# An attention-and-two-MoE kernel on one core: one subtraction put ahead of a weight decode, and three operand splits per token pair put earlier

## The chip, the cores and the metric

The kernel runs on 1 core of one Trainium2 chip. The metric is the device time of one execution in microseconds (us). The engines are called by the names of the profile: PE (TensorE, matmuls), PEld (its weight loads), DVE (VectorE), ACT (ScalarE), POOL (GpSimd) and SP (SyncE, which issues most transfers). Each engine works through its own queue in the order in which the program issues instructions.

## The reference

```python
def _attn_ref(q, k, v, alpha):            # 4 x 8 heads, 768 steps, 48 wide
    for t in range(S):
        state = alpha[:, :, t, :, None] * state + np.einsum('bhd,bhe->bhde', k[:, :, t], v[:, :, t])
        y[:, :, t] = np.einsum('bhd,bhde->bhe', q[:, :, t], state)

def _moe_ref(x, w_in, w_out):             # 3072 x 384, 384 x 2048, 2048 x 384
    h = x @ w_in
    return (h * sigmoid(h)) @ w_out

def _moe2_ref(x, w_gate, w_val, w_out):   # 384 x 1536 twice, 1536 x 384
    g = x @ w_gate
    return (g * sigmoid(g) * (x @ w_val)) @ w_out
```

The output of the attention is the x of the first layer, whose result is the x of the second.

## The kernel before, in words

**Precision.** Matmuls run on fp32r operands. To keep fp32 accuracy an operand is split in a high part (an ACT copy that rounds to fp32r) and a low part (a subtraction source minus high, `sub`, line 321). A product of two split operands is three matmuls: high by high, low by high, high by low.

**First phase (to about 537 us).** Chunks of 128 tokens go through the attention; seven blocks of 3 or 4 chunks go through the first layer in steps (j, f) of block j and 128 hidden columns f. Each step has `g1` (line 721 to 724: h = x times w_in), `act1` (line 733: ACT computes silu twice, line 738 into the high part gh and line 739 in place into the PSUM bank h; the low part gl = h - gh is a DVE subtraction, issued by the `rest` that act1 returns) and `g2` (lines 770, 771 with gh, then 773 with gl). The weights arrive as 64-bit numbers and are decoded on DVE in three instructions (lines 93, 98, 103), rounded on ACT (line 702), and their low part is subtracted on POOL for the first six units and on DVE from then on (`low_unit`). One call of `units1` (line 1298) pushes one unit through one stage each of this chain. Steps are software-pipelined: g1 of step s + 1 is issued ahead of g2 of step s.

**Second phase.** The second layer works on three pairs of 512-token blocks (p = 0, 1, 2). Its gate and value products use a bilinear scheme with 15 products instead of 18 for a 3 by 2 tile of blocks, in eight groups a pair (even groups gate, odd groups value). A group's products p0 to p14 are three matmuls each (line 1095) into accumulators A to K, one PSUM bank each; DVE merges (line 1106) add banks and saved copies in between. For example `"h": ("H", "D", ALU.add, 1)` is H = D + temps 1, and products p10 and p13 both add to D, one before and one after that merge; `"k2"` is K = temps 3 - E, and product p11 then adds to K. In a gate group the operations u0 to u5 are a silu on ACT (line 1122), in a value group the product of the value with that silu on DVE (line 1127), which leaves a tile a per hidden block f and token block b.

**Output.** For each of the 24 (f, b) of a pair, `osplit` (line 1137) makes the high part of a on ACT (line 1147) and the low part on DVE (line 322, by `sub`), and `og` (line 1149) issues nine matmuls (line 1158) with weights from a ring. Operands 0, 1, 3, 4, ... take tiles of the tags gh and gl, two buffers each, which the silus of the second phase also use; every third operand (2, 5, ...) takes the one tile of tag y3. `output` (line 1164) copies finished sums into a tile of tag big2 and writes them out.

**Order of the second phase.** Nothing is reordered by a scheduler: the constants GATE, VALUE, OUTPUT, SPLIT and MOVING give each operation a due time in a scale of 192 per pair and 15 per group, all events are sorted by it (line 1202), and `run` issues them in this order to every engine's queue. The due times are not microseconds. In pair 0 the events around the change are, in order: u2 of group 6 (92.56, ACT), s12 (93.39, ACT), h7 (94.81, an ACT copy for the next pair), C4 of group 6 (95.36, DVE), u4 of group 6 (95.47, ACT, reads what C4 wrote), u5 of group 6 (96.75, ACT), then of group 7 h (97.25, DVE), p13 (98.12), p4 (98.42), u0 (98.46, DVE), g (99.15, DVE), k (100.76, DVE), u3 (101.26, DVE), p3 (101.30), k2 (101.33, DVE), p6, p8, t (102.01, DVE), h9 (102.05, ACT, next pair), u1 (102.14, DVE), p11 (102.34), u2 (102.54, DVE), the high and low part of operand 0 (102.55), p1 (103.21), those of operand 1 (103.89), og 0 (105.43), s11, C4, u4, C5, u5 (108.30 to 110.59), the high and low part of operand 2 (111.12), of operand 3 (112.71), og 1 and og 2 (112.82, 112.83). Pairs 1 and 2 have the same order, 192 and 384 later; pair 2 has no copies for a next pair.

Of the kernel before, what the change touches and what calls it, by code (L numbers as in the profile page):

```python
# [11 lines left out]
F32R = mybir.dt.float32r  # L12
# [49 lines left out]
SPLIT = (  # L62
    102.55, 103.89, 111.12, 112.71, 118.27, 118.43, 119.02, 126.43, 129.94, 131.62, 132.60, 135.86, 138.65,
    143.41, 148.72, 149.46, 154.12, 157.35, 162.20, 163.22, 165.39, 165.58, 174.69, 175.51,
)
MOVING = (
# [202 lines left out]
def fast(ctx, tc, pk, w1, w2, out, bad_i):  # L269
# [5 lines left out]
    blocks1, n = [], 0  # L275
# [20 lines left out]
    mp = ctx.enter_context(tc.tile_pool(name="mp", bufs=2))  # L296
# [24 lines left out]
    def sub(eng, lo, src, hi):  # L321
        eng.tensor_tensor(out=lo, in0=src, in1=hi.bitcast(F32), op=ALU.subtract)  # L322
# [403 lines left out]
    def g1(s):  # L726
        j, f = steps[s]
        w = len(blocks1[j]) * C
        h_t[j, f] = bank(s % 2, f"h{j}_{f}")[:, :w]
        xk = [(x_t[j][:, 0, k, :w], x_t[j][:, 1, k, :w]) for k in range(KT)]  # L730
        product(h_t[j, f], unit_t["1", 2 * f], xk)

    def act1(j, f):
        w = len(blocks1[j]) * C
        hb = h_t.pop((j, f))
        gh = mp.tile([128, 512], F32R, tag="gh", name=f"gh{j}_{f}")[:, :w]
        gl = mp.tile([128, 512], F32R, tag="gl", name=f"gl{j}_{f}")[:, :w]
        ACT.activation(out=gh, in_=hb, func=AF.Silu)  # L738
        ACT.activation(out=hb, in_=hb, func=AF.Silu)  # L739
        act_t[j, f] = (gh, gl)  # L740

        def rest():
            sub(DVE, gl, hb, gh)

        return rest
# [57 lines left out]
    def load_x1(p):  # L803
        r = x1r_t[p] = big(0, f"x1r{p}").rearrange("p (b k t) -> p b k t", b=2, k=KT)
        for b in range(2):
            t = 1024 * p + 512 * b
            SP.dma_start(out=r[:, b], in_=x1_d[:, :, t:t + 512])

    def moving(p, op, eng=None):

        x = x1r_t[p].rearrange("p b k t -> p (b k) t")
        if op[0] == "a":
            out, a, alu, b = SUMS[op]
            (eng or DVE).tensor_tensor(out=x[:, out], in0=x[:, a], in1=x[:, b], op=alu)
            return
        i = int(op[1:])
        if op[0] == "h":
            t = mov[i] = pools2["s"].tile([128, 2, 512], F32R, tag=f"mov{i}", name=f"mov{p}_{i}", bufs=1)
            ACT.activation(out=t[:, 0], in_=x[:, SOURCE[i]], func=AF.Copy)
        else:  # L820
            sub(eng or DVE, mov[i][:, 1], x[:, SOURCE[i]], mov[i][:, 0])
# [313 lines left out]
    o_t, ahl, ob_t, result = {}, {}, {}, {}  # L1135

    def osplit(p, n, low):
        f, b = order[n]
        if low:
            ah, al = ahl[f, b]  # L1140
            return sub(DVE, al, a_t.pop((f, b)), ah)
        if n % 3 == 2:
            y = mp.tile([128, 2, 512], F32R, tag="y3", name=f"ahl{p}_{n}", bufs=1)
            ahl[f, b] = y[:, 0], y[:, 1]
        else:
            ahl[f, b] = [mp.tile([128, 512], F32R, tag=t, name=f"{t}{p}_{n}") for t in ("gh", "gl")]
        ACT.activation(out=ahl[f, b][0], in_=a_t[f, b], func=AF.Copy)  # L1147

    def og(p, n):
        f, b = order[n]  # L1150
        if f == 0:
            for m in range(KT):
                hold((p, b, m), f"o{p}_{b}_{m}", 1)
            o_t[b] = [held[p, b, m][1] for m in range(KT)]
        ah, al = ahl.pop((f, b))
        for m in range(KT):
            for i, (l, x) in enumerate(((0, ah), (1, ah), (0, al))):
                PE.matmul(  # L1158
                    o_t[b][m], part(ring_t[p, f], m, l), x, start=(f == 0 and i == 0),
                    stop=(f == NF2 - 1 and i == 2),  # L1160
                )
        used(p, NG2 + f // 5)

    def output(p, b, m):
        t = 1024 * p + 512 * b
        if b == 0 and m == 0:
            ob_t[p] = mp.tile([128, 2, KT, 512], F32, tag="big2", name=f"ob{p}", bufs=1)
        ob, src = ob_t[p][:, b], o_t[b][m]
        rows = slice(m * 128, (m + 1) * 128)
        end = p == NPAIR - 1 and b  # L1170
        if end and m == 0:
            result["bad"] = nc.values_load(bad_i[0:1, 0:1], min_val=0, max_val=128)
        if end and m == KT - 1:
            ACT.activation(out=ob[:, m, :256], in_=src[:, :256], func=AF.Copy)
            DVE.tensor_copy(ob[:, m, 256:], src[:, 256:])
            for i, eng in enumerate((ACT, SP)):
                cs = slice(256 * i, 256 * i + 256)
                eng.dma_start(out=out[rows, t + cs.start:t + cs.stop], in_=ob[:, m, cs])
        else:
            if m % 2:  # L1180
                DVE.tensor_copy(ob[:, m], src)
            else:
                ACT.activation(out=ob[:, m], in_=src, func=AF.Copy)
            SP.dma_start(out=out[rows, t:t + 512], in_=ob[:, m])
        release((p, b, m))

    events = []
    for p in range(NPAIR):
        t0 = PAIR * p
        for n in range(NG2):  # L1190
            events += [(t0 + GROUP * n + t, lambda a=(p, n, op): group_op(*a)) for op, t in (GATE, VALUE)[n % 2]]
        for n, (f, b) in enumerate(order):
            events.append((t0 + OUTPUT[n], lambda a=(p, n): og(*a)))
            events.append((t0 + SPLIT[n], lambda a=(p, n, 0): osplit(*a)))
            events.append((t0 + SPLIT[n] + 0.004, lambda a=(p, n, 1): osplit(*a)))
            if f == NF2 - 1:
                for m in range(KT):
                    events.append((t0 + OUTPUT[n] + 0.002 + 0.001 * m, lambda a=(p, b, m): output(*a)))
        if p + 1 < NPAIR:
            events.append((t0 + 3 * GROUP, lambda a=p + 1: load_x1(a)))  # L1200
            events += [(t0 + t, lambda a=(p + 1, op): moving(*a)) for op, t in MOVING]
    events.sort(key=lambda e: e[0])
# [95 lines left out]
    def units1(ahead=4, top=NU1):  # L1298


        up_to("s1", st["h1"] - 1, lambda u: low_unit(("1", u), DVE if u >= 6 else POOL), NU1)
        up_to("h1", st["f1"] - 1, lambda u: high_unit(("1", u), wp, "w"), NU1)
        up_to("e1", st["d1"] - 1, lambda u: decode_unit(("1", u), 1), NU1)
        up_to("d1", st["d1"], lambda u: decode_unit(("1", u), 0), min(top, st["l1"]))
        up_to("f1", st["e1"] - 1, lambda u: decode_unit(("1", u), 2), NU1)
        up_to("l1", st["d1"] + ahead - 1, load1, NU1)
# [61 lines left out]
    steps = turns + [(0, f) for f in range(FB, NF1)]  # L1368
    steps += [(j, f) for j in range(2, NB1) for f in range(NF1)]

    due, n = [first] * (2 * len(turns)), first
# [93 lines left out]
    units1()  # L1465
    attn(1, False)
    g1(0)
    rest = act1(*steps[0])
    units1()
    rest()  # L1470
    for s, (j, f) in enumerate(steps):
        need1(2 * f + 1)
        if s == 0:
# [1 line left out]
        n = 19 + 2 * (s + 3 - len(steps))  # L1475
# [25 lines left out]
@with_exitstack  # L1501
def tile_kernel(ctx, tc, pk, w1, w2, out):
    nc = tc.nc
    fp = ctx.enter_context(tc.tile_pool(name="fp", bufs=1))
    bad128 = fp.tile([128, 1], I32, name="bad128")
    with ExitStack() as inner:
        inner.enter_context(tc.manual_schedule())
        rv = fast(inner, tc, pk, w1, w2, out, bad128)
    with tc.If(rv > 0):
        general(tc, pk, w1, w2, out)  # L1510
# [70 lines left out]
```

## Time and profile before

| | |
|---|---|
| median of 3 runs | 937.41 us (936.27 to 938.69) |
| time of the profiled execution | 938.12 us |
| its span, first to last instruction | 936.3 us |
| mean granted TensorE clock | 0.992 |
| PE / PEld busy | 98% / 83% |
| DVE / ACT / POOL busy | 66% / 48% / 31% |
| chain that ended last | PE 89%, DVE 5%, issue 2% |

Times in a timeline row are the start and the duration in us; "xN" is the number of instructions merged into the row, and the brackets at its end give the idle time of the engine ahead of it and what ended it. Instructions of one engine are pipelined, so the next one may start before the last has ended. Ends of matmuls are modelled, starts are recorded.

### The profile page before, as it was taken

The page shows a single profiled execution, that of the slowest core. Times are in us where ns is not written, and L with a number is a line of the kernel's source. Part 1 is how long each engine was busy: PE and PEld are TensorE (multiplying, and loading weights), DVE is VectorE, ACT ScalarE, POOL GpSimd, SP SyncE. Part 2 cuts the span into 40 slices and gives each one's busy share as a digit, 9 for nine tenths or more (in the row PEclk, how much of TensorE's full clock was granted, in tenths as well). Part 3 has the DMA queues.
Part 4 walks back from the last instruction along what each step waited for, and adds up shares of the span by engine and source line. Part 5 has one row for each costly group of instructions (what it writes and reads, how often), then busy time and mean ns, then how long its engine had stood idle before and what let it go on. Part 6 is the DMA issues. An engine that isn't in the chain of part 4 may idle for free.

```text
span 936.3 us, 14380 instructions
## 1 busy us (share of the span) xinstructions
PE 915.2 (98%) x5210; PEld 779.6 (83%) x5210; DVE 618.1 (66%) x1107; ACT 453.0 (48%) x1019; POOL 287.9 (31%) x401
## 2 busy tenths in 40 slices
PE   9989999999999999999999999999999999999996
PEld 5669998889999998988888888878888888888785
DVE  8889936656577668465268366786477875577732
ACT  3545435646465565555346344543544454444432
POOL 5430006528779789686228000000000000000000
PEclk9899999999999999999999999999999999999998
DMA  7854203243645554532375486532757503755302
GB/s 235 300 187 153 85 1 105 80 142 119 194 160 194 167 175 161 181 108 101 118 264 208 157 299 224 185 114 85 244 213 267 194 10 135 269 205 214 121 0 71
DMA packets 43007, 150.89 MB, mean 161 GB/s; under 512 B 4400, under 2 KB 9008, under 8 KB 40240
## 3 DMA queue, kind: packets, MB, share of 16 engines
q1 hardware_dynamic: 42304, 149.30, 46.3%
q8 instruction: 43, 0.70, 0.3%
q10 hardware_dynamic: 624, 0.59, 0.2%
q14 instruction: 36, 0.29, 0.1%
HBM read 118.03 MB, written 29.88 MB: 158 GB/s over the span
## 4 chain that ended last, share of the span: by engine, by line
PE 89%; DVE 5%; issue 2%; DMA 1%; POOL 1%; ACT 1%; SPq 0%; ACTq 0%; POOLq 0%; DVEq 0%
PE o L1158 15%; PE h L721 7%; PE x L773 7%; PE x L770 7%; PE x L771 7%; PE h L722 7%; PE h L724 7%; PE A L1095 5%; PE D L1095 5%; PE E L1095 5%; PE yd L562 2%; PE K L1095 2%; PE F L1095 2%; PE C L1095 2%; PE B L1095 2%; PE G L1095 2%
## 5 line engine op out<-in xcount | busy, mean ns | idle before, releaser
L322 DVE TENSOR_TENSOR gl<-h,gh 128x384 fp32r<-128x384 f32 (+1 forms) x112 | 68.5, 612 | 89.8 <-ACT h L739 84.4
L721 PE MATMUL h<-x,w 128*128 128x384 f32 (+1 forms) x336 | 122.7, 365 | 1.8 <-DMA x<-y 1.8
L770 PE MATMUL x<-gh,w 128*128 128x384 f32 (+1 forms) x336 | 121.5, 362 | 0.4 <-ACT gh L738 0.4
L771 PE MATMUL x<-gh,w 128*128 128x384 f32 (+1 forms) x336 | 121.2, 361 | 0.0
L722 PE MATMUL h<-x,w 128*128 128x384 f32 (+1 forms) x336 | 120.9, 360 | 0.0
L738 ACT ACTIVATE gh<-h 128x384 fp32r<-128x384 f32 (+1 forms) x112 | 59.9, 534 | 105.3 <-PE h L724 103.4
L1158 PE MATMUL o<-gh,ring 128*128 128x512 f32 x288 | 88.8, 389 | 0.0
L773 PE MATMUL x<-gl,w 128*128 128x384 f32 (+1 forms) x336 | 84.5, 359 | 1.6 <-DVE gl L322 1.6
L724 PE MATMUL h<-x,w 128*128 128x384 f32 (+1 forms) x336 | 84.3, 358 | 0.0
L420 POOL TENSOR_TENSOR kq<-in,r 128x256 f32<-128x256 f32 x47 | 43.0, 915 | 130.1 <-DVE rc L419 76.3
L721 PEld LDWEIGHTS h<-x,w 128*128 128x128 f32 x336 | 63.1, 188 | 10.6 <-issue 5.4
L770 PEld LDWEIGHTS x<-gh,w 128*128 128x128 f32 x336 | 63.1, 188 | 6.7 <-ACT gh L738 1.1
L773 PEld LDWEIGHTS x<-gl,w 128*128 128x128 f32 x336 | 61.3, 188 | 8.1 <-DVE gl L322 2.3
L771 PEld LDWEIGHTS x<-gh,w 128*128 128x128 f32 x336 | 63.1, 188 | 5.2
L722 PEld LDWEIGHTS h<-x,w 128*128 128x128 f32 x336 | 63.1, 188 | 5.1
L724 PEld LDWEIGHTS h<-x,w 128*128 128x128 f32 x336 | 61.3, 188 | 5.9
L1158 PEld LDWEIGHTS o<-gh,ring 128*128 128x128 f32 x288 | 54.1, 188 | 11.2
L739 ACT ACTIVATE h<-h 128x384 f32<-128x384 f32 (+1 forms) x112 | 59.5, 532 | 0.0
L322 DVE TENSOR_TENSOR gl<-a,gh 128x512 fp32r<-128x512 f32 x48 | 32.9, 692 | 37.3 <-ACT gh L1147 36.2
L1158 PE MATMUL o<-gl,ring 128*128 128x512 f32 x144 | 56.4, 392 | 0.8 <-DVE gl L322 0.8
L1095 PE MATMUL A<-mov,ring 128*128 128x512 f32 x198 | 55.7, 389 | 0.0
L1095 PE MATMUL D<-mov,ring 128*128 128x512 f32 x198 | 55.6, 389 | 0.0
(211 smaller groups left out, 1983.3 us busy)
## 6 DMA issues: line engine op xcount, KB each, us to landing
ring<-comb_d SPq DMA_DIRECT2D x21, 1920.0 KB, 7.7
raw<-in_w_dram SPq DMA_DIRECT2D x58, 384.0 KB, 4.4
in<-in_pk_dram SPq DMA_DIRECT2D x22, 770.5 KB, 4.4
ring<-wo_d SPq DMA_DIRECT2D x6, 1920.0 KB, 7.3
comb_d<-area SPq DMA_DIRECT2D x8, 896.0 KB, 5.4
in_v<-in_pk_dram SPq DMA_DIRECT2D x24, 256.0 KB, 3.7
comb_d<-area SPq DMA_DIRECT2D x8, 640.0 KB, 4.9
x1r<-x_d SPq DMA_DIRECT2D x6, 768.0 KB, 8.9
```

Of the source, the lines that this page charges most:

```text
L322: eng.tensor_tensor(out=lo, in0=src, in1=hi.bitcast(F32), op=ALU.subtract)
L420: KF(d).tensor_tensor(out=kq_t[d][:, 0], in0=in_t[n][1][:, 0, ps_], in1=r_t[d][:, :, 1:], op=ALU.mult)
L721: PE.matmul(acc, part(u, k), xh, start=(k == 0), stop=False)
L722: PE.matmul(acc, part(u, k, 1), xh, start=False, stop=False)
L724: PE.matmul(acc, part(u, k), xl, start=False, stop=(k == len(xk) - 1))
L738: ACT.activation(out=gh, in_=hb, func=AF.Silu)
L739: ACT.activation(out=hb, in_=hb, func=AF.Silu)
L770: PE.matmul(x1_t[j][m], part(u, m), gh, start=(f == 0), stop=False)
L771: PE.matmul(x1_t[j][m], part(u, m, 1), gh, start=False, stop=False)
L773: PE.matmul(x1_t[j][m], part(u, m), gl, start=False, stop=(f == NF1 - 1))
L1095: PE.matmul(acc, s(hs, r), x[:, hx], start=op in new and i == 0, stop=i == 2, skip_group_check=True,)
L1158: PE.matmul(o_t[b][m], part(ring_t[p, f], m, l), x, start=(f == 0 and i == 0), stop=(f == NF2 - 1 and i == 2),)
```

## The change

In the first phase, `rest` of the first step (its gl subtraction) is issued right behind the two silus, ahead of a call of `units1` instead of behind it. In the second phase, the splits of operands 0, 1 and 2 of every pair get due times of their own, high and low apart, and their six parts go to slices of a tile of tag big2, the tag that the results take later, instead of tiles of tags gh, gl and y3.

```diff
+FIRST_SPLITS = ((96.0, 97.0), (98.0, 99.3), (100.0, 101.2))
...
-        if n % 3 == 2:
+        if n < 3:
+
+            if n == 0:
+                ob_t[p] = mp.tile([128, 6, 512], F32R, tag="big2", name=f"ahl{p}", bufs=1)
+            ahl[f, b] = ob_t[p][:, 2 * n], ob_t[p][:, 2 * n + 1]
+        elif n % 3 == 2:
...
-            events.append((t0 + SPLIT[n], lambda a=(p, n, 0): osplit(*a)))
-            events.append((t0 + SPLIT[n] + 0.004, lambda a=(p, n, 1): osplit(*a)))
+            high, low = FIRST_SPLITS[n] if n < 3 else (SPLIT[n], SPLIT[n] + 0.004)
+            events.append((t0 + high, lambda a=(p, n, 0): osplit(*a)))
+            events.append((t0 + low, lambda a=(p, n, 1): osplit(*a)))
...
-    rest = act1(*steps[0])
+    act1(*steps[0])()
     units1()
-    rest()
```

## Rows read from the trace of the kernel before

**Rows 1.** The page, part 1: busy us, share of the span, instructions.

```profile
PE 915.2 (98%) x5210; PEld 779.6 (83%) x5210; DVE 618.1 (66%) x1107; ACT 453.0 (48%) x1019; POOL 287.9 (31%) x401
```

**Rows 2.** PE's waits: us in total, times, longest us.

```profile
PE x L773 <- DVE gl L322: 1.6, 1, 1.6
...
PE o L1158 <- DVE gl L322: 0.8, 3, 0.3
```

**Rows 3.** Timeline of DVE, 60.5 to 70 us.

```profile
63.30 0.55 DVE L98 SCALAR_TENSOR_TENSOR raw<-raw,dec 128x384 int32<-128x384 int32 x1
...
64.16 1.38 DVE L103 SCALAR_TENSOR_TENSOR raw<-raw 128x384 int32<-128x384 int32 x1
65.46 0.68 DVE L322 TENSOR_TENSOR gl<-h,gh 128x512 fp32r<-128x512 f32 x1
...
67.64 0.55 DVE L103 SCALAR_TENSOR_TENSOR raw<-raw 128x384 int32<-128x384 int32 x1
```

**Rows 4.** Timeline of all engines, 50 to 67 us.

```profile
62.78 0.59 ACT L739 ACTIVATE h<-h 128x512 f32<-128x512 f32 x1
...
64.03 1.10 POOL L322 TENSOR_TENSOR w<-raw,w 128x384 fp32r<-128x384 f32 x1 [4.38 <-ACT w L702]
...
64.20 0.40 PE L771 MATMUL x<-gh,w 128*128 128x512 f32 x1
...
66.19 0.97 PE L773 MATMUL x<-gl,w 128*128 128x512 f32 x3 [1.60 <-DVE gl L322]
```

**Rows 5.** Timeline of all engines, 113 to 127 us.

```profile
117.38 0.19 PEld L770 LDWEIGHTS x<-gh,w 128*128 128x128 f32 x1 [0.34 <-ACT gh L738]
...
118.03 0.55 DVE L322 TENSOR_TENSOR gl<-h,gh 128x384 fp32r<-128x384 f32 x1
...
118.63 0.47 PEld L773 LDWEIGHTS x<-gl,w 128*128 128x128 f32 x3 [0.26 <-DVE gl L322]
```

**Rows 6.** A stretch: length, busy PE, PEld, DVE, ACT, POOL, clock, DMA, GB/s.

```profile
110.00:120.00 10.00, 9.97 (x53) 8.87 (x52) 9.83 (x22) 4.92 (x11) 0.00 (x0) 1.00 0.00 0
```

**Rows 7.** Timeline of all engines, 598 to 622 us (pair 0).

```profile
608.17 0.70 DVE L1106 TENSOR_TENSOR H<-D,temps 128x512 f32<-128x512 f32 x1 [0.18 <-PE D L1095]
...
608.91 0.63 ACT L1122 ACTIVATE sg<-temps 128x512 f32<-128x512 f32 x1
...
609.25 0.84 PE L1095 MATMUL D<-mov,ring 128*128 128x512 f32 x3
...
611.50 0.70 DVE L1106 TENSOR_TENSOR K<-temps,E 128x512 f32<-128x512 f32 x1
...
612.65 0.84 PE L1095 MATMUL K<-mov,ring 128*128 128x512 f32 x3
...
614.01 0.61 PE L1158 MATMUL o<-gh,ring 128*128 128x512 f32 x2
614.14 1.29 DVE L322 TENSOR_TENSOR gl<-a,gh 128x512 fp32r<-128x512 f32 x2
...
618.18 0.63 ACT L1147 ACTIVATE ahl<-a 128x512 fp32r<-128x512 f32 x1 [3.31 <-DVE a L1127]
...
618.85 0.69 DVE L322 TENSOR_TENSOR ahl<-a,ahl 128x512 fp32r<-128x512 f32 x1 [0.76 <-ACT ahl L1147]
...
621.32 0.62 PE L1158 MATMUL o<-gh,ring 128*128 128x512 f32 x2
```

**Rows 8.** Timelines of ACT and of PE, 864 to 885 us (pair 2).

```profile
872.10 0.62 ACT L1122 ACTIVATE sg<-temps 128x512 f32<-128x512 f32 x1
...
872.84 0.84 PE L1095 MATMUL D<-mov,ring 128*128 128x512 f32 x3
...
877.60 0.61 PE L1158 MATMUL o<-gh,ring 128*128 128x512 f32 x2
...
884.89 0.39 PE L1158 MATMUL o<-gh,ring 128*128 128x512 f32 x1
```

**Rows 9.** The instructions on tile x1e: durations in ns, first and last start.

```profile
L751 SPq DMA_DIRECT2D x_d<-x1e x7: 572/579/617, 148.2 to 540.0; - x7
```

## The prediction, made before the changed kernel was run

> **What bounds the kernel now.** I read the page's busy times first: the matmul row of TensorE (PE) fills 98% of the span [rows 1]. A change off PE's path is therefore worth at most what PE waits, and a change that makes PE wait costs in full, since nothing later has room to win it back. Next came the waits of PE alone: x (line 773) waits once for the VectorE (DVE) subtraction gl, 1.60 us, and o (line 1158) three times for gl, 0.8 us in all [rows 2]. These are the two places that the diff touches.
>
> The second figure is too small, because an end of a pipelined matmul is modelled. Starts are exact. In pair 0, products D start at 609.25 and K at 612.65, five products of three matmuls later, so 15 matmuls take 3.40 us, 0.227 each. The first three output operands, 27 matmuls, would take 6.12; from 614.01 to 621.32 they take 7.31 [rows 7]. So 1.19 us are lost there: before the first low part, and at operand 2, whose split comes late. Pair 2 takes 877.60 to 884.89, or 7.29, so 1.17 [rows 8]; pair 1 repeats pair 0 to 0.01. **What the second edit can win is 1.19 + 1.19 + 1.17 = 3.55 us.** For the first edit, x line 773 would have started 0.23 behind the last line 771, at 64.43; it starts at 66.19 [rows 4], and the three matmuls then take 0.97 where three take 0.84 without a wait [rows 4, 7]: 1.76 + 0.13 = 1.89 us. The 0.13 is what I charge for every restart after a wait.
>
> **Edit 1: gl of step 0 ahead of the decode.** No instruction is added. On DVE, gl (65.46) trades places with one decode triple that starts at 63.30 [rows 3]. ACT's h ends at 62.78 + 0.59 = 63.37 [rows 4]; with 0.05 for the handover (gl ends 66.14, PE starts 66.19) gl starts at 63.42 and ends at 64.10, before PE wants it at 64.43. That wait goes. What is late next? DVE is in order and runs on from this decode with hardly a gap: from 110 to 120 us it is still busy 9.83 of 10 us [rows 6], the last of five such stretches from 70 on with 9.83 to 9.86, and PE waits for it there. The weight load of x line 770 stands 0.34 us for ACT's gh, which is queued behind the rounding of a unit that DVE decoded; that of line 773 stands 0.26 us for gl, which starts at 118.03 because DVE has got no further [rows 5]. A permutation at the head of a queue that never empties does not change when its 118.03 entry runs. PE gets ahead by up to 1.89 us at 66 and gives it all back by 118.63. What is left is the 0.12 us that DVE stands idle from 63.30 to 63.42. Cost of edit 1: **+0.1 us**. Bounds: up to 0.83 us gained, if a collision with POOL disappears (below), and 0.3 lost, if one grows.
>
> **Edit 2: the splits.** Three ACT copies and three DVE subtractions a pair are moved, none added. No DMA is among them and nothing moves on POOL's or SP's queue. The tile big2 costs nothing: before pair 0 its last user was x1e, whose last transfer is issued at 540.0 [rows 9], some 69 us ahead of the split; in pairs 1 and 2 it is the last pair's result tile, written out long before. The results of the same pair allocate big2 again behind operand 23 or so, when operands 0 to 2 have been read.
>
> Where the moved work stands in the queues decides. In the order of due times the first high part (96.0) falls on ACT between u4 (95.47) and u5 (96.75) of group 6; the first low part (97.0) falls on DVE between C4 (95.36) of group 6 and h (97.25) of group 7. So h, with everything after it on DVE, now waits for that ACT copy. PE waits for h: product p13 adds to D, which h reads first.
>
> Pair 0, step by step [rows 7]:
> - The high part takes u5's place on ACT, 608.91. A low part starts 0.67 after its high part (618.18, 618.85): 609.58. DVE would have started h at 608.17.
> - Back to back DVE starts one such instruction every 0.60 (two gl, 1.29 with the second at its own 0.69). So h starts at 610.18, ends 0.70 later at 610.88, and p13 starts at 610.93 instead of 609.25: PE stands 1.68, plus 0.13.
> - Between h and k2 DVE now has u0, g, the second low part, k, the third low part and u3 (their high parts follow u5 on ACT at once, in time): k2 starts seven places after h, 610.18 + 4.20 = 614.38, and ends 0.70 later. Before it started at 611.50.
> - Product K (p11) adds to what k2 writes, so it starts at 615.13 instead of 612.65. That is 2.48 in all, the 1.81 of the first stall included, plus a restart: **2.61 us**.
> - The output then runs unbroken; its three operands are ready: **-1.19**. The banks it takes were last read by u4, u0 and u3, the latest ending near 614.5, before PE gets there.
>
> Net +1.42, and the same in pair 1. In pair 2 no copy for a next pair stands in ACT's queue, so the high part starts at 872.10 [rows 8], the low part at 872.77, h at 873.37, k2 at 877.57, ending 878.27; K starts at 878.32 instead of 872.84 + 3.40 = 876.24. That is 2.08 + 0.13 = 2.21, less 1.17: +1.04. Behind u2 the DVE merges and the split of operand 3 come later too, but operand 3 is needed only 6.12 us into the output and its low part ends more than 1 us ahead, so I cost that at nothing.
>
> **Sum:** 1.42 + 1.42 + 1.04 + 0.1 = 3.98, about +4.0 us. The profiled execution took 938.12 us (span 936.3 and 1.8 around it), 0.71 above the median 937.41. Against its own time it gives 942.1; against the median, **941.4 us**.
>
> A rule to weigh at edit 1. A decode of line 103 takes 1.38 us when POOL's low part starts at 64.03 beside it, and 0.55 us at 67.64 [rows 3, 4]: 0.83 for a collision. With gl first, POOL still starts at 64.03, as gl is ending, and meets the decode behind it, so I keep the collision. The Trainium skill (SBUF — State Buffer, "Who interferes with whom") says that a port pair shared by VectorE and GpSimd belongs to whichever instruction started first, and that a VectorE instruction with at most one SBUF input stays out of it. By that rule gl, which reads h from PSUM, could run beside POOL unharmed, and edit 1 would win about 0.7 us if one of POOL's two instructions came to lie beside a gl; the sum would be 3.15. The two durations above agree with the rule; no row shows which instruction will meet which.
>
> **The rivals.**
> - *The early splits are hidden* (faster). If the first low part did not hold up h, DVE would do the three where it stands idle, and both output waits would go: -3.55 + 0.1, 934.0 us, or about 932 if edit 1 kept its 1.89 too. For it: ACT has room, and the output operands lie ready well before. Against it: DVE stands idle only 0.18 us ahead of h [rows 7], so it has no room at that place, and the queue order is fixed by the due times. It decides at h: only if the low part started by 608.17 - 0.60 = 607.57 would h keep its time, and the ACT copy starts at 608.91. Chance 0.09.
> - *Only the first stall comes* (no change). If DVE caught up before k2, PE would lose only p13's wait, 1.81, 1.81 and 1.41 in pair 2 (h ending 874.07), less 3.55, plus 0.1: +1.6, 939.0. It would take a DVE spacing of 0.5 where rows give 0.60. Chance 0.08.
> - *Edit 1 keeps its gain* (no change). If PE's waits at 117 and 118 came from something that moves along with PE, 1.89 would stay: 3.88 - 1.89 = +2.0, 939.4. Against it stands the full DVE queue [rows 6]. Chance 0.07.
> - *A collision with POOL goes* (slower, by less): one of POOL's two low parts comes to lie beside a gl, and a decode is spared its 0.83 [rows 3]: 3.98 - 0.83 = 3.15, 940.6. It decides whether POOL's second low part falls beside the gl of step 1. Chance 0.06.
>
> **How the numbers follow.** A measurement of this kernel can tell about 0.3%, 2.8 us, from no change. My forecast, +4.0, has 0.70; its own range is 940.6 to 942.6, edit 1's bounds and the scatter of the runs included. With the last rival, slower has 0.76. The two middle rivals give no change 0.15, and the first gives faster 0.09. The range 938.9 to 942.6 takes in all but the first rival and the edges.
>
> **What would show it.** Right: in each pair a new wait of PE D (line 1095) for DVE H (line 1106), near 1.7, 1.7 and 1.3 us, and one of PE K for DVE K, near 0.7; DVE's ahl subtraction ahead of H, idle before it on ACT; operands 0 to 2 in 6.12 us; no wait of x line 773 at 66, but line 773 again near 118.7. Wrong: H starting before the first low part, D p13 without a wait, or PE well ahead of 118.6 at that step.

## The result, and the profile after

The changed kernel takes 942.81 us (median of 5 runs, 941.25 to 943.34). The kernel before, timed beside it and with two more runs than the prediction had, takes 938.22 (936.27 to 938.69). The ratio is 1.0053 [1.0036, 1.0071]: slower by half a per cent. The forecast was 941.4, slower, with a range that ends at 942.6. The sign, the size of the effect and the places are as forecast; the measured median lies 0.2 us above the range.

Busy time hardly moves, since the change moves instructions and adds none. Part 1 and the first line of part 4 of the page after:

```profile
PE 916.4 (97%) x5210; PEld 780.3 (83%) x5210; DVE 616.8 (66%) x1107; ACT 452.3 (48%) x1019; POOL 288.0 (31%) x401
PE 82%; DVE 10%; issue 3%; DMA 2%; ACT 1%; POOL 1%; SPq 0%; ACTq 0%; POOLq 0%; DVEq 0%
```

DVE had 5% of the chain before and has 10% now, for a loss of half a per cent: the chain is followed back through whatever released a wait, so a short new wait can turn a long stretch of it onto another engine. What was lost is told by the waits of PE after (us in total, times, longest us):

```profile
PE D L1096 <- DVE H L1107: 4.1, 3, 1.5
...
PE K L1096 <- DVE K L1107: 1.8, 3, 0.6
...
PE A L1096 <- DMA ring<-comb_d: 0.3, 1, 0.3
```

Both waits of [rows 2] are gone: x no longer waits for gl, and o waits for nothing. In their place stand, three times each, the two waits that the prediction named, D for H and K for k2, and one for a transfer of the weight ring that it did not name. (Lines after are one or a few higher: 1095 is now 1096, 1106 is 1107, 1147 is 1153, 773 is 774.)

Pair 0 of the kernel after, timeline of all engines, 604 to 628 us, answers to [rows 7]:

```profile
607.59 0.84 PE L1096 MATMUL D<-mov,ring 128*128 128x512 f32 x3
...
609.28 0.63 ACT L1153 ACTIVATE ahl<-a 128x512 fp32r<-128x512 f32 x1
...
609.94 0.69 DVE L323 TENSOR_TENSOR ahl<-a,ahl 128x512 fp32r<-128x512 f32 x1 [1.58 <-ACT ahl L1153]
...
610.55 0.69 DVE L1107 TENSOR_TENSOR H<-D,temps 128x512 f32<-128x512 f32 x1
...
611.29 0.96 PE L1096 MATMUL D<-mov,ring 128*128 128x512 f32 x3 [1.51 <-DVE H L1107]
...
614.75 0.68 DVE L1107 TENSOR_TENSOR K<-temps,E 128x512 f32<-128x512 f32 x1
...
615.57 0.93 PE L1096 MATMUL K<-mov,ring 128*128 128x512 f32 x3 [0.59 <-DVE K L1107]
...
617.04 6.28 PE L1164 MATMUL o<-ahl,ring 128*128 128x512 f32 x27
...
623.16 0.62 PE L1164 MATMUL o<-gh,ring 128*128 128x512 f32 x2
```

This is the whole mechanism in nine rows: DVE stands idle 1.58 us for the ACT copy of operand 0, H starts behind the subtraction, PE stands for H, then for k2, and then the 27 matmuls of operands 0 to 2 run in one piece, which they did not do before.

To weigh it, take exact starts: from product p10 (the D at 607.59) to the first matmul of operand 3 (623.16) is 15.57 us. Before, p10 started at 607.22 and that matmul at 621.32 [rows 7], which is 14.10. The row of before that starts the measure:

```profile
607.22 0.84 PE L1095 MATMUL D<-mov,ring 128*128 128x512 f32 x3
```

The same measure, before and after:

| pair | before | after | measured | predicted |
|---|---|---|---|---|
| 0 | 14.10 | 15.57 | +1.47 | +1.42 |
| 1 | 14.10 | 15.58 | +1.48 | +1.42 |
| 2 | 14.09 | 15.19 | +1.10 | +1.04 |
| sum | | | **+4.05** | +3.88 |

The first edit is read in the same way, on another stretch: from the DVE instruction ahead of the first decode (an addition into `state`) to the x with gl that started at 118.63 [rows 5]. Before, from the timeline of DVE:

```profile
63.03 0.36 DVE L651 TENSOR_TENSOR state<-yd,state 128x192 f32<-128x192 f32 x1
```

That makes 55.60. After, from the timelines of DVE and of PE:

```profile
63.38 0.36 DVE L652 TENSOR_TENSOR state<-yd,state 128x192 f32<-128x192 f32 x1
63.76 0.69 DVE L323 TENSOR_TENSOR gl<-h,gh 128x512 fp32r<-128x512 f32 x1
...
119.08 0.80 PE L774 MATMUL x<-gl,w 128*128 128x384 f32 x3
```

119.08 - 63.38 is 55.70: **+0.10**, which is what the prediction charged for DVE's pause ahead of gl. It repeats: the stretch takes 55.57 to 55.62 us in the seven profiles of kernels that lack the first edit and have DVE's queue full, and 55.70 to 55.72 in the four that have the first edit and a full queue. The wait at 66 is gone, and PE waits instead a little in many places, as the weight loads (PEld) of the kernel after show:

```profile
69.30 0.53 PEld L774 LDWEIGHTS x<-gl,w 128*128 128x128 f32 x3 [0.23 <-DVE gl L323]
...
72.90 0.47 PEld L774 LDWEIGHTS x<-gl,w 128*128 128x128 f32 x3 [0.30 <-DVE gl L323]
...
117.82 0.19 PEld L771 LDWEIGHTS x<-gh,w 128*128 128x128 f32 x1 [0.45 <-ACT gh L739]
...
119.08 0.47 PEld L774 LDWEIGHTS x<-gl,w 128*128 128x128 f32 x3 [0.25 <-DVE gl L323]
```

The spans differ by 4.7 us (941.0 against 936.3). Of these 0.35 are there before either edit acts (63.38 against 63.03), 0.10 come from the first edit, 4.05 from the pairs and 0.54 from the ring transfer, read from two starts of A products of which the second waits for it, both from the timeline of PE after:

```profile
810.18 0.84 PE L1096 MATMUL A<-mov,ring 128*128 128x512 f32 x3
...
813.40 0.94 PE L1096 MATMUL A<-mov,ring 128*128 128x512 f32 x3 [0.34 <-DMA ring<-comb_d]
```

They lie 3.22 apart. Before, from the timeline of all engines:

```profile
806.80 0.84 PE L1095 MATMUL A<-mov,ring 128*128 128x512 f32 x3
...
809.52 0.89 PE L1095 MATMUL A<-mov,ring 128*128 128x512 f32 x3
```

They lay 2.72 apart, and the second took 0.89 where others take 0.84, so the waiting cost about 0.05 before; 0.50 is new by the starts, and 0.54 with the slower group behind the wait. The four terms give 5.04, and the last matmul does start 5.0 later. The other 0.3 is won behind it, in the last copies and their transfer: the span ends 8.81 us after the start of the last matmul before (927.51) and 8.48 after (932.52).

### The profile page after: what moved, and what is told of

Read it like the earlier page. It is cut to its first block, busy times and chain, and to the rows that moved or that the text cites. A ratio compares the mean times of both kernels' runs of the same rounds, so it can differ in the third digit from the quotient of the medians.

```text
span 941.0 us, 14351 instructions
## 1 busy us (share of the span) xinstructions
PE 916.4 (97%) x5210; PEld 780.3 (83%) x5210; DVE 616.8 (66%) x1107; ACT 452.3 (48%) x1019; POOL 288.0 (31%) x401
## 4 chain that ended last, share of the span: by engine, by line
PE 82%; DVE 10%; issue 3%; DMA 2%; ACT 1%; POOL 1%; SPq 0%; ACTq 0%; POOLq 0%; DVEq 0%
PE o L1164 16%; PE h L722 6%; PE x L771 6%; PE x L772 6%; PE x L774 6%; PE h L723 6%; PE h L725 6%; PE A L1096 5%; PE E L1096 5%; PE D L1096 5%; PE yd L563 2%; PE K L1096 2%; PE C L1096 2%; DVE raw L99 2%; PE F L1096 1%
## 5 line engine op out<-in xcount | busy, mean ns | idle before, releaser
L739 ACT ACTIVATE gh<-h 128x384 fp32r<-128x384 f32 (+1 forms) x112 | 59.9, 535 | 106.0 <-PE h L725 104.6
L1164 PE MATMUL o<-gh,ring 128*128 128x512 f32 x252 | 77.5, 389 | 0.0
L1164 PE MATMUL o<-ahl,ring 128*128 128x512 f32 x270 | 65.1, 389 | 0.0
L1164 PEld LDWEIGHTS o<-ahl,ring 128*128 128x128 f32 x270 | 50.7, 188 | 10.6
L323 DVE TENSOR_TENSOR gl<-a,gh 128x512 fp32r<-128x512 f32 x42 | 29.0, 692 | 41.0 <-ACT gh L1153 39.8
```

What stands on the lines that cost most here:

```text
L1164: PE.matmul(o_t[b][m], part(ring_t[p, f], m, l), x, start=(f == 0 and i == 0), stop=(f == NF2 - 1 and i == 2),)
```

## The experiments

**The theory.** Low part 0 stands in DVE's queue ahead of h, its high part is not ready, and the delay reaches PE at p13 and again at p11; the first edit is worth nothing because DVE's queue of decodes stays full until about 118 us. Rivals: the loss comes from the first edit, or from the tile big2; the first edit wins, and something else takes more; the splits can't be hidden anywhere.

**1. The first edit alone** (on the kernel before):

```diff
-    rest = act1(*steps[0])
+    act1(*steps[0])()
     units1()
-    rest()
```

> The first edit alone. Theory (DVE's full queue sets PE's pace until about 118 us): no gain, 0 to +0.2 us. The wait of x for gl near 66 us is gone, but PE waits again for gl in the next steps and near 118, and the time from the first matmul of h (58.13 before) to the x<-gl matmul behind the gl at 118.03 (118.63 before) stays at 60.5 to 60.7 us. Rival (the 1.89 us stay won): that time falls to about 58.6 us and the kernel gains 1.9 us, which would mean that the second edit costs 6.5 and not 4.6.

Measured: 937.28 against 937.73, ratio 0.9995 [0.9982, 1.0008]. The stretch from the state instruction to that x (61.25 to 116.95) takes 55.70, the same +0.10. The first edit alone changes nothing that can be measured. From the first matmul of h, the point that the expectation used, the stretch takes 61.14, outside its 60.5 to 60.7; that point is a poor one (see experiments 8 and 9). This profile has a ring wait as well, 0.4 us, without the second edit.

**2. The second edit alone** (the kernel after with those lines put back).

> The second edit alone. Theory: +3.9 us (1.42 + 1.42 + 1.04 by pair), with the same three waits of D for H (PE idle 1.5, 1.5, 1.1) and of K for K (0.6 each) as in the changed kernel. Rival (the first edit wins 1.9): +6.5 us. Besides, near 809 us before, a ring transfer lands just as PE wants it: if the extra 0.6 us in the changed kernel's profile is scatter of that transfer, it need not show here; if the second edit causes it, the wait of A for the ring shows again with about 0.3 us of PE idle.

Measured: 940.71 against 937.73, 1.0033 [1.0021, 1.0045]. The pairs take 15.56, 15.56 and 15.16, +4.0 in all, and the waits of PE are those of the kernel after:

```profile
PE D L1096 <- DVE H L1107: 4.1, 3, 1.5
...
PE K L1096 <- DVE K L1107: 1.7, 3, 0.6
...
PE x L774 <- DVE gl L323: 1.6, 1, 1.6
PE A L1096 <- DMA ring<-comb_d: 1.1, 1, 1.1
```

So the second edit makes the loss, by itself and at the places named; the medians differ by 3.0, a microsecond less than the pairs. The wait of x for gl is back, at no cost. The ring wait is 1.1 us here: it differs from profile to profile.

**3. The same splits, put where DVE is idle** (on the second edit alone). Before, DVE stood idle 1.94 us in group 5, ahead of an F merge. The six parts get due times there; the tile big2 stays. Timeline of DVE before, 583 to 586 us:

```profile
585.61 0.70 DVE L1106 TENSOR_TENSOR F<-D,temps 128x512 f32<-128x512 f32 x1 [1.94 <-ACT temps L1102]
```

```diff
-FIRST_SPLITS = ((96.0, 97.0), (98.0, 99.3), (100.0, 101.2))
+FIRST_SPLITS = ((55.0, 58.0), (56.1, 58.1), (56.2, 58.2))
```

> The kernel before with the second edit's tile, but the three high parts due at 55.0 to 56.2 and the three low parts at 58.0 to 58.2, ahead of the merge f of group 5, where DVE stands idle 1.94 us and three low parts take 1.8. Theory (where the low parts stand in DVE's queue is all that costs): no wait of D or K, operands 0 to 2 in 6.12 us per pair instead of 7.31, -3.55 us, about 934.7 against 938.2. Rival (the big tile or the early copies cost by themselves, or the time saved is lost at another wait): 0 or slower.

Measured: 933.44 against 937.73, **0.9955 [0.9941, 0.9969]**, faster than both kernels. The waits for H, for k2 and of o are all absent, and each pair takes 12.92, that is -1.18 against before. The timeline of all engines of this kernel, 575 to 619 us:

```profile
579.47 0.62 ACT L1153 ACTIVATE ahl<-a 128x512 fp32r<-128x512 f32 x1
579.66 1.29 DVE L1107 TENSOR_TENSOR temps<-D,temps 128x512 f32<-128x512 f32 x2 [0.65 <-PE D L1096]
580.89 1.15 ACT L1153 ACTIVATE ahl<-a 128x512 fp32r<-128x512 f32 x2
...
581.66 1.89 DVE L323 TENSOR_TENSOR ahl<-a,ahl 128x512 fp32r<-128x512 f32 x3
583.69 0.70 DVE L1107 TENSOR_TENSOR F<-D,temps 128x512 f32<-128x512 f32 x1
...
612.10 6.28 PE L1164 MATMUL o<-ahl,ring 128*128 128x512 f32 x27
```

The three subtractions fill 581.66 to 583.55, and F, which followed an idle 1.94 us, now follows them with no wait shown. So big2 costs nothing, the 3.55 us that the prediction took as the second edit's most (here 3.53 by the pairs, 4.3 by the medians) are there to be had, and what decides is the place in the queue.

**4. Experiment 3 with the first edit** (the same due times in the kernel after).

> The same early splits with the first edit. Theory: -3.4 us, not apart from the early splits alone. Rival (the first edit wins 1.9): -5.4 us.

Measured: 934.54 against 937.73, 0.9962 [0.9946, 0.9978], 1.1 us above experiment 3, with intervals that overlap. With the late splits gone, too, the first edit gains nothing.

**5. Operand 0 alone split early** (on the second edit alone; both places where `n < 3` decides say `n < 1`).

> The second edit for operand 0 alone (high at 96.0, low at 97.0); operands 1 and 2 split as before. Theory: p13 still waits for h in every pair (PE idle 1.5, 1.5, 1.1), but k2 is now behind one low part and not three, so K does not wait: PE is 1.81, 1.81 and 1.41 us late. Of the output's loss 0.53 goes (the low part of operand 0) and about 0.6 at operand 2 stays: operands 0 to 2 take 6.7 us. Sum 1.28 + 1.28 + 0.88 = +3.4 us. Rival (each early low part costs its own third of the loss): +1.5 us.

Measured: 941.45 against 937.31, 1.0055 [1.0032, 1.0078]. As expected, H waits in full (4.1 us in three waits of PE) and K not at all: the first low part makes the first stall, the other two make the second. The size is a miss. The pairs take +1.37, +1.40 and +1.27, 4.04 in all where 3.4 was expected, since operand 2, back at its old place, waits longer than before, most of all in pair 2. Timeline of all engines, 604 to 628 us:

```profile
617.57 0.63 ACT L1153 ACTIVATE ahl<-a 128x512 fp32r<-128x512 f32 x1 [2.88 <-DVE a L1128]
...
618.26 2.62 PE L1164 MATMUL o<-ahl,ring 128*128 128x512 f32 x9 [0.18 <-ACT ahl L1153]
```

ACT stands idle ahead of its copy, for a DVE product (`a`), and DVE is late because of the low part in front of h. The delay of one instruction reached a third wait behind it, which I had not followed.

**6. High parts early, low parts behind u2** (on the second edit alone).

```diff
-FIRST_SPLITS = ((96.0, 97.0), (98.0, 99.3), (100.0, 101.2))
+FIRST_SPLITS = ((96.0, 102.55), (98.0, 103.89), (100.0, 103.9))
```

> The second edit with its tile and its early high parts, but with the low parts due at 102.55, 103.89 and 103.90, behind u2. Theory: no wait of D or K; the low part of operand 0 comes as late as before (0.53 lost), operand 2 no longer waits for the tile y3 (0.59 won): -1.8 us, operands 0 to 2 in about 6.7 us. Rival (the copies on ACT or the tile hold DVE or PE up): the waits of D or K stay and it is slower.

Measured: 935.93 against 937.31, 0.9987 [0.9972, 1.0001]. No wait for H or k2 is left, and one of o for the first low part, 0.3 us, stays in each pair. The pairs take 13.47, -0.63 each, 1.9 in all, as expected; by the runs it is a gain of 1.4 us that can hardly be measured. The early ACT copies harm nothing. It is the low parts ahead of h that cost.

**7. Low part 0 just behind h** (on the second edit alone; 97.3 in place of 97.0).

```diff
-FIRST_SPLITS = ((96.0, 97.0), (98.0, 99.3), (100.0, 101.2))
+FIRST_SPLITS = ((96.0, 97.3), (98.0, 99.3), (100.0, 101.2))
```

> The second edit with the low part of operand 0 due at 97.3 instead of 97.0, so behind h and no longer ahead of it; all else as in the second edit alone. Theory: D does not wait; DVE now stands for the high part behind h, so g comes 0.9 us late in pairs 0 and 1 and 0.5 in pair 2 and E (p3) waits for it, then K for k2: PE late by 2.0, 2.0 and 1.6, less 1.19, 1.19 and 1.17: +2.1 us. Rival (the early low parts cost the same wherever they stand among these merges): +4.0 as the second edit.

Measured: 939.16 against 937.25, 1.0017 [1.0007, 1.0028]. One place further back and the wait of D is gone; the next merges pay instead. Waits of PE:

```profile
PE K L1096 <- DVE K L1107: 2.2, 3, 0.7
PE E L1096 <- DVE G L1107: 1.8, 3, 0.7
```

The pairs take +0.89, +0.89 and +0.49, 2.27 where 2.1 was expected. Timeline of all engines, 602 to 622 us:

```profile
606.89 0.70 DVE L1107 TENSOR_TENSOR H<-D,temps 128x512 f32<-128x512 f32 x1 [0.17 <-PE D L1096]
...
608.29 0.69 DVE L323 TENSOR_TENSOR ahl<-a,ahl 128x512 fp32r<-128x512 f32 x1 [0.71 <-ACT ahl L1153]
...
610.25 0.97 PE L1096 MATMUL E<-mov,ring 128*128 128x512 f32 x3 [0.75 <-DVE G L1107]
```

The same ACT copy holds DVE for 0.71 us, now between h and g, and product E waits for g. Of the places tried in this stretch, only the one behind u2 (experiment 6) holds up no merge that PE waits for.

**8 and 9. Is a full DVE queue what eats the first edit?** From unit 6 on, the low part of a first-layer weight unit is taken off DVE: ACT writes zeros in its place, so these kernels leave out the contribution of those low parts to the first layer. Experiment 8 is the kernel before with that alone, experiment 9 has the first edit too.

```diff
+    def low_fill(key):
+        u = unit_t[key]
+        ACT.activation(out=u[:, DM:], in_=raw_t.pop(key), func=AF.Copy, scale=0.0)
...
-        up_to("s1", st["h1"] - 1, lambda u: low_unit(("1", u), DVE if u >= 6 else POOL), NU1)
+        up_to("s1", st["h1"] - 1, lambda u: low_fill(("1", u)) if u >= 6 else low_unit(("1", u), POOL), NU1)
```

> The kernel before, without the low parts of the first layer's weight units from 6 on: where DVE subtracted them, ACT writes zeros. DVE's queue between 70 and 121 us is so 0.47 us shorter per unit. Theory: the waits of PE near 117 and 118 go, the wait of x for gl near 66 stays; from the first matmul of h to the matmul of x that started at 118.63 it takes 0.4 to 0.6 us less than before, 59.9 to 60.1. Rival (these waits are ACT's or PE's own): 60.5 or more.

> The same without the low parts, and with the first edit. Theory (the first edit's gain is lost only because DVE's queue is full): now it is kept in part; the next gl, behind six decodes that stay on DVE, comes at the same time as before, so about 1.0 us (0.8 to 1.2) of the 1.89 stays won: 58.9 to 59.1 us from the first matmul of h to that matmul of x. Rival (the first edit is worth nothing for another reason): as without the edit, 59.9 to 60.1.

Measured, one run each: 939.28 and 936.79. By the reference point of the expectations, the first matmul of h, the stretch takes 60.04 (59.9 to 60.1 was expected) and 59.29 (58.9 to 59.1 was), so 0.75 apart. That point is a poor one, because the granted clock around it differs between profiles (below). From the state instruction, after which DVE's queue sets the pace, it takes 55.17 and 54.32 (63.38 to 118.55, 61.78 to 116.10), and 55.60 and 55.70 with the low parts on DVE. So the edit that costs 0.10 with a full queue wins 0.85 with a relieved one. The first is what the prediction said; the second is less than the 1.89 that the wait at 66 was worth. Where the rest goes can be read step by step. The table has starts of the first x with gl of a step, counted from the state instruction, as differences in us: after and experiment 1 against before, experiment 9 against experiment 8.

| start before | after | experiment 1 | 9 against 8 |
|---|---|---|---|
| 3.17 (the wait at 66) | -0.85 | -1.75 | -1.76 |
| 6.95 | -0.98 | -1.04 | -1.00 |
| 10.27 | -0.75 | -0.76 | -0.85 |
| 13.93 | -0.35 | -0.36 | -0.85 |
| 24.39 | -0.24 | -0.24 | -0.85 |
| 38.31 | -0.07 | -0.10 | -0.85 |
| 55.60 (the one at 118) | +0.10 | +0.10 | -0.85 |

So PE does get ahead by 1.75 (by 0.85 in the profile after, where it was still at work on h and on x with gh). Some 0.9 of it goes within two steps whether the queue behind is relieved or not; the rest is lost bit by bit where the queue is full, and stays won to the last 0.01 where it is not.

**10. The changed kernel once more**, beside a new set of runs of the kernel before.

> The changed kernel once more, beside the kernel before on one chip. Theory (the queue order costs 4.05 us, the first edit 0.10, and what lay above that was scatter of a ring transfer and of the runs): +3.5 to +4.8 us, and in the profile 1.47, 1.48 and 1.10 us more per pair from product D ahead of the output to the fourth operand, whatever the wait of A for the ring near 813 us is. Rival (a cost that the trace of queues does not hold): above +4.8 again.

Measured: 941.23 against 937.25, 1.0046 [1.0027, 1.0064]. The pairs take 15.58, 15.59 and 15.19, +4.1, and no ring wait is in the list. The loss of the pairs repeats to 0.1 us; the total moves by 1.6 from one set of runs to the next.

**11. The kernel before once more**, for the ring transfer.

> The kernel before once more, for its profile. Theory: the transfer into the ring near 809 us is a matter of scatter: 2.72 us between the two groups of A there without a wait, 2.7 to 3.3 with it, in either kernel. Pairs as before: 14.10 us from product D to the fourth operand. Rival: never above 2.75 without the second edit's delays.

Measured: 943.21 in one run at a mean granted clock of 0.982 (0.992 in the first profile of before), so its total is of no use here. The stretch of the two A products takes 2.72, without a wait, and the pairs 14.10 each, as in the first profile of before.

## Why the prediction was right, and where it failed

**The queue order (right).** Low part 0 ahead of h, and h bound to the ACT copy. In pair 0, p10 starts 0.37 us later after than before (607.59 against 607.22). With that added, the prediction's steps say 609.28 for the high part, 609.95 for the low part, 610.55 for h and 611.30 for p13; the timeline has 609.28, 609.94, 610.55 and 611.29. k2 was put at 614.75 and started at 614.75. K was put at 615.50 and started at 615.57. Experiment 7 shows that one place in the queue decides this, and experiment 3 that the same instructions elsewhere cost nothing.

**The stalls (right, a little small).** p13 was to lose 1.68 and lost 1.67; the first output was to start 2.61 later and started 2.66 later (617.04 against 614.01, less 0.37). The output was to win 1.19 and did: operands 0 to 2 take 6.12 (617.04 to 623.16). The small miss is in the handover from k2 to K, charged with 0.05: k2 ends at 615.43 (614.75 and 0.68) and K starts at 615.57, 0.14 later. The restart behind it was charged with 0.13 and cost 0.11 (617.04 - 615.57 is 1.47, and 614.01 - 612.65 was 1.36 before).

**Pair 2 (right).** Its smaller stall, +1.04 forecast and +1.10 measured, rests on the ACT queue without copies for a next pair.

**The first edit (right).** +0.1 forecast, +0.10 measured, and experiments 1, 4, 8 and 9 say why: PE gets ahead at 66, and what is left of that after two steps is eaten where DVE's queue is full. The place of the collision held too. POOL starts at 64.38, 0.35 later like everything there, as gl ends, and meets the decode. Timeline of DVE and POOL after, 63 to 70 us:

```profile
64.37 0.55 DVE L99 SCALAR_TENSOR_TENSOR raw<-raw,dec 128x384 int32<-128x384 int32 x1
64.38 1.42 POOL L323 TENSOR_TENSOR w<-raw,w 128x384 fp32r<-128x384 f32 x1 [4.38 <-ACT w L703]
64.95 1.07 DVE L94 TENSOR_SCALAR dec<-raw 128x384 int32<-128x384 int32 x1
...
67.16 1.07 POOL L323 TENSOR_TENSOR w<-raw,w 128x384 fp32r<-128x384 f32 x1 [1.36 <-ACT w L703]
67.26 1.39 DVE L104 SCALAR_TENSOR_TENSOR raw<-raw 128x384 int32<-128x384 int32 x1
```

Two decodes are stretched, 1.07 and 1.39, as two were before [rows 3 show one of them, 1.38]. No decode was spared, so the rival by which a collision goes is refuted. By the Trainium skill (SBUF — State Buffer, "Who interferes with whom") the instruction that issues first holds the shared ports and the other blocks. The rows agree: line 99 starts 0.01 ahead of POOL and keeps its 0.55, and POOL takes 1.42; from the end of line 99 (64.92) to its own end (65.80) it runs 0.88. The other half of the rule as the prediction words it, that an instruction with at most one SBUF input stays out, does not hold for line 94: it reads one tile from SBUF and takes 1.07 behind POOL, against 0.36 alone. The same section of the Trainium skill excepts VectorE's 2-port perf modes, which the prediction leaves out; no row shows in which mode line 94 ran. Whether gl would stay out is shown by no row here, since it shares only 0.07 us with POOL (64.38 to 64.45).

**The other rivals.** "Only the first stall comes" is refuted by the wait of K in all three pairs. "Edit 1 keeps its gain" is refuted by experiment 1. "The early splits are hidden" is false for this place and true for the one of experiment 3; its 934.0, reckoned for the edit as it stands, is near what experiments 3 and 4 gave (933.44 and 934.54).

**What failed** is a size and not the mechanism: the sum that gives 941.4, and the range laid round it, "its own range is 940.6 to 942.6, edit 1's bounds and the scatter of the runs included". The measured 942.81 is also the time of the profiled execution, so the two profiles say what makes up the 1.41 us above the forecast.

- The base, 0.71: I counted from a median of three runs, 937.41, though the profiled execution, 938.12, gave 942.1. With five runs the median is 938.22. Later sets of 15 to 24 runs put it at 937.25 to 937.73, so 937.41 was near the usual time and the 0.71 is scatter.
- The pairs, 0.17: charged with 3.88, measured 4.05. Edit 1 cost the 0.10 that it was charged with.
- A transfer that lands just in time, put at nothing by having no term: the ring's, which cost about 0.05 before and 0.54 more after.
- The start and the end of the span, which neither edit touches: 0.35 lost and 0.33 won.

Without the first or the third of these the median would have lain inside; 942.6 is only 1.2 us above the forecast. That is too little for the scatter. The runs of before alone reach over 2.4 us (936.27 to 938.69), and the medians of the nine comparisons here lie from 1.0 below to 0.5 above what their own pairs and first edit add up to. The second set of the same two kernels, 941.23 against 937.25 (+3.98), would have lain inside; that the first did not is within this scatter.

The ring transfer is issued 6.61 us ahead of the first of the two A products in all 13 profiles, so neither edit moves its issue. What differs is how long it takes: 9.15 us before, 9.69 after, 8.86 to 10.50 over all. The two A products lie 3.23 apart with the first edit alone, 4.03 with the second alone, 3.02, 3.17 and 3.05 in experiments 3, 4 and 7, and 2.72 to 2.79 in the others, the second profile of the changed kernel among them. The three profiles without either edit (before, 8 and 11) stay at 2.72 to 2.75. So why the transfer takes longer in some profiles stays open, and that the edits have a part in it is not excluded.

## What to carry to other kernels

Work that is moved in an in-order queue belongs where that queue stands idle, and its operand must be ready there; how early the result is wanted says nothing. Three low parts put ahead of a merge that PE waits for cost 4 us, and the same three in an idle 1.94 us, some 26 us earlier, win 3.5. A wait that ends ahead of a queue that stays full comes back further down that queue, so measure from start to start over the whole full stretch before you count its removal as a gain. And a range needs the base's own scatter, and a term for transfers that land just in time.

## What the runs showed that I had not expected

The granted clock fell early in the profile after, lower than in the profile before, and that difference cost nothing. Windows of the kernel after (length, busy PE, PEld, DVE, ACT, POOL, granted clock, DMA share, GB/s):

```profile
55.00:60.00 5.00, 4.73 (x50) 3.75 (x49) 4.50 (x9) 2.61 (x9) 2.69 (x2) 0.50 0.59 225
60.00:65.00 5.00, 5.00 (x20) 4.00 (x19) 3.57 (x9) 2.90 (x7) 0.62 (x2) 0.87 0.28 62
```

Before, the same windows had 0.76 and 1.00. At 0.50, the level of 1.2 GHz, the matmuls of h start 0.43 us apart, against 0.23 before; yet h is ready 0.34 us after the state instruction starts in both, and the decode queue sets the pace from there. The 0.35 us by which that instruction came later were there at 15 us, with the clock at 1.00 in both: a DVE scan into g starts at 15.00 before and at 15.35 after.

Over all profiles a lower clock in this part does go with lost time, ahead of both edits. Windows of experiment 1, of before and of experiment 11:

```profile
35.00:60.00 25.00, 20.66 (x220) 15.60 (x220) 21.64 (x42) 12.81 (x48) 9.66 (x11) 0.93 0.62 219
35.00:60.00 25.00, 21.42 (x212) 16.05 (x211) 21.31 (x42) 11.78 (x44) 9.98 (x11) 0.80 0.62 225
35.00:60.00 25.00, 23.32 (x170) 16.82 (x170) 17.92 (x37) 10.36 (x41) 7.30 (x9) 0.55 0.62 224
```

The state instruction starts at 61.25, 63.03 and 66.65 in them; the other ten, at 0.75 to 0.86, lie at 61.48 to 63.38, without a strict order. This is the largest scatter that the profiles show in any part compared here. It is also why experiments 8 and 9 should not have been counted from the first matmul of h, which lies in this part.

The other surprise is how exactly a collision adds up. Where POOL's low part meets a DVE instruction that started first, it ends 0.88 us after that instruction in the two cases above: 64.92 to 65.80, and 67.35 (the end of a line 94 that started at 66.99 and took 0.36) to 68.23. In every such meeting between 58 and 72 us of the 13 profiles it is 0.87 to 0.90.
